# Chunk 1's row transposes moved from TensorE and ScalarE's queue to SyncE's queue, and one subtraction moved ahead of a bias

## The chip, the cores and the metric

One core of one Trainium2 chip runs the whole program. The metric is the time of one execution on the device in microseconds (us). The kernel before took 767.68 us, the median of four runs (767.52 to 768.24). A profile of a further execution is the source of all other times below.

## What is computed

The reference is one transformer layer on a sequence of 2048 rows of 1024 columns in bf16: a layer norm, attention in which each position looks at eight positions at a distance of two, an output projection and a residual sum, then a second layer norm, a bilinear gated block (gate times up, then down) and a residual sum.

```python
S, D, H, Dh, W, dil, F = 2048, 1024, 32, 32, 8, 2, 3584
h  = x + attention(layernorm(x) @ wqkv) @ wo     # 8 keys per position, 2 apart, softmax over the 8
n  = layernorm(h)
h2 = h + ((n @ w_gate) * (n @ w_up)) @ w_down
```

## The kernel before

**Tiling.** The 2048 rows are cut into four chunks (`c` = 0 to 3) of 512 rows, and a chunk into four tiles (`t`) of 128 rows. A tile of rows lies with the rows on the 128 partitions. The matmuls need the normalized rows turned, with the columns on the partitions: `lnT1_c` is that turned copy of one chunk, 128 partitions by 8 blocks by 512 rows. A product of 128 output columns with a chunk is a group of eight 128x512 matmuls (`mm_group`), which the program plans at 1.73 us (`GROUP_US`).

**Order.** [...] The class `Background` holds generators of side work (norms, attention). After each matmul group `bg.step(GROUP_US)` adds that much credit, and the generators emit work and `yield` its planned cost until the credit is used up. A yield of 0.45 that goes away therefore lets the next piece of side work be emitted a little sooner.

**The start.** Chunk 0 is normalized and turned on TensorE (`first_transpose`), and its query, key and value projections begin (`qkv(0, [1, 2])`, then `qkv(0, [3])`, line 489 for the matmuls). In these three blocks of four groups each, the generator `rows_gen` normalizes chunk 1 and then chunk 2. For chunk 1 it also turns the rows. Tiles 0 and 1 go through `transpose_on_array`: eight 128x128 transposes on TensorE into two PSUM tiles `ptb` (line 245), then one copy to SBUF on ScalarE and one on VectorE (line 247). Tiles 2 and 3 go through `transpose` with ScalarE's queue as the issuer: one DMA transpose each (line 236). Right after `qkv(0, [3])` comes `qkv(1, [2])`, whose first matmul needs all four turned tiles of chunk 1. The load of the queries for attention (`load_qk`, line 516) is made to wait for the last turned tile too.

**SyncE's queue.** SyncE issues the loads of weights and rows, and the stores of the projections to DRAM: `qd` for the queries (line 395), `kd` and `vd` for keys and values (line 415). `sg` is the SBUF tile that ScalarE fills from PSUM for each store. [...] The normalized rows live in four buffers (pool `ln`), so that the rows of chunk 2 can only be written when the transposes of chunk 1 have read theirs.

**The down projection.** Late in the kernel the down projections of chunks 0 and 1 are computed by a seven-product scheme: `F11`, `F12`, `F22` are sums of activations, `b12`, `b21`, `t2`, `t4` sums and differences of halves of the down weights, each of 14 blocks of 128x512 in two tiles. `dprod` runs one quarter (`q`) of such a product (14 matmuls, line 1108), `put` adds it to the residual and stores it (line 805). `t_half(dst, x0, x1, a)` subtracts one tile of half the weights on VectorE (line 1101). Beside this, chunks 2 and 3 get their second layer norm: `ln_stat` on VectorE, `rstd_of` on ScalarE (lines 190 and 191), the bias `nbs[3]` on VectorE (line 1351), and then `ln_rows`, one ScalarE pass for each tile (line 1197) with a DMA transpose behind it (line 1198). `zs[q]` are the accumulators that the product with `t4` goes on adding to once `put` has read them.

Of the kernel before, what the change touches and what calls it, by code (L numbers as in the profile page):

```python
# [8 lines left out]
BF = mybir.dt.bfloat16  # L9
# [16 lines left out]
TC = 512  # L26
NCH = S // TC
SUB = TC // 4
KO = D // 128
# [49 lines left out]
def kernel(  # L79
# [11 lines left out]
    nc = tc.nc  # L91
# [8 lines left out]
    lnTp = ctx.enter_context(tc.tile_pool(name="lnT", bufs=3))  # L100
# [5 lines left out]
    psum = ctx.enter_context(tc.tile_pool(name="psum", bufs=8, space=PSUM))  # L106
# [82 lines left out]
    def rstd_of(mv4, rs4, lo, hi):  # L189
        nc.scalar.activation(rs4[:, lo:hi], mv4[:, lo:hi, 1], ACTF.Ln, bias=eps[:])  # L190
        nc.scalar.activation(rs4[:, lo:hi], rs4[:, lo:hi], ACTF.Exp, scale=-0.5)
# [21 lines left out]
    lnTs = {}  # L213
# [3 lines left out]
    class Norm1:  # L217
# [11 lines left out]
        def norm(self, t):  # L229
            self.lns[t] = normalize(xtiles[self.c][t], self.mv4, self.rs4, t)  # L230

        def transpose(self, t, eng=nc.sync):
            c = self.c
            if c not in lnTs:
                lnTs[c] = lnTp.tile([128, KO, TC], BF, tag="lnT", name=f"lnT1_{c}")
            eng.dma_start_transpose(lnTs[c][:, :, bass.ts(t, 128)], self.lns[t][:])

        def transpose_on_array(self, t):
            c = self.c
            if c not in lnTs:  # L240
                lnTs[c] = lnTp.tile([128, KO, TC], BF, tag="lnT", name=f"lnT1_{c}")
            for hf in range(2):
                pt = psum.tile([128, KO // 2, 128], BF, tag="mm", name=f"ptb{c}_{t}_{hf}")
                for kk in range(KO // 2):
                    nc.tensor.transpose(pt[:, kk, :], self.lns[t][:, bass.ts(4 * hf + kk, 128)], ident[:])
                copy = nc.vector.tensor_copy if hf else nc.scalar.copy
                copy(lnTs[c][:, bass.ts(hf, 4), bass.ts(t, 128)], pt[:])

    def rows_gen(n, on_array):
        for t in range(6):  # L250
            if t < 4:
                n.stat(t)
                yield 1.5
            if 0 < t < 5:
                n.norm(t - 1)
                yield 0.55
            if t > 1 and on_array:
                if t < 4:
                    n.transpose_on_array(t - 2)
                    yield 0.45  # L260
                else:
                    n.transpose(t - 2, nc.scalar)

    class NormOnScalar(Norm1):

# [80 lines left out]
    ident = const.tile([128, 128], BF)  # L346
# [131 lines left out]
    xtiles[2] = load_x(2, "x", nc.sync)  # L478
    norm1 = {1: Norm1(1), 2: Norm1(2), 3: NormOnScalar(3)}
    bg.add(rows_gen(norm1[1], True))  # L480
    rows2 = rows_gen(norm1[2], False)
    bg.add(rows2)
    for j in range(4):
# [615 lines left out]
    def sub(dst, x0, x1, eng=nc.vector):  # L1099
        for d, a0, a1 in zip(dst, x0, x1):  # L1100
            eng.tensor_tensor(f16(d[:, 0:NH, :]), f16(a0[:, 0:NH, :]), f16(a1[:, 0:NH, :]), ALU.subtract)
# [25 lines left out]
    b11, b21 = ([wts["dn", n, a] for a in range(2)] for n in ("11", "21"))  # L1127

    def halves(parts, name):
        return [pool.tile([128, KO, TC], BF, tag=tag, name=f"{name}{i}") for i, (pool, tag) in enumerate(parts)]  # L1130
# [37 lines left out]
    def ln_stat(c, t):  # L1168
        stats(hss[c][t], ln2[c][0], t)
# [42 lines left out]
    def t_half(dst, x0, x1, a):  # L1212
        sub([dst[a]], [x0[a]], [x1[a]])
# [58 lines left out]
    t2 = halves(((wpool, "w"), (wpool, "w")), "t2_")  # L1272
# [21 lines left out]
    b21 = halves(((lnTp, "lnT"), (lnTp, "lnT")), "b21r")  # L1294
# [53 lines left out]
    t4 = t2  # L1348
    ln_stat(3, 3)
    rstd_of(ln2[3][0], ln2[3][1], 0, 4)  # L1350
    nc.vector.scalar_tensor_tensor(nbs[3], ln2[3][0][:, :, 0], -1.0, ln2[3][1][:], ALU.mult, ALU.mult)
    t_half(t4, b21, t2, 0)
    l3 = lnTp.tile([128, KO, TC], BF, tag="lnT", name="lnT2_3")
    t_half(t4, b21, t2, 1)
    for q in range(4):
# [162 lines left out]
```

## Time and profile before

| What | Value |
|---|---|
| median of four runs | 767.68 us (767.52 to 768.24) |
| the profiled execution | 768.31 us, of which its span is 766.1 us |
| busy: TensorE, VectorE, ScalarE, GpSimd | 756.6, 626.7, 532.7, 144.6 us |
| granted TensorE clock, as a share of full speed | 0.999 |
| two sets of eight transposes of chunk 1 on TensorE | start at 24.12 and 26.29 us |
| two DMA transposes of chunk 1 from ScalarE's queue | issue from 31.03 us, 2.77 us in all |

All times inside the profile count from the start of the span. A line of a timeline has the start, the duration, the engine, the source line, the operation, the tile written and the tiles read, how many there were, and in brackets how long the engine had idled before and what ended that. A name with a q behind it (SPq, ACTq) is the engine's instruction queue that issues a DMA. In the list of waits the numbers are the total, how often, and the longest, in us. The line of a DMA issue ends with the median time from issue to landing in us.

### The profile page before, as it was taken

How to read it: one execution, taken by the hardware profiler on the slowest of the kernel's cores; microseconds unless marked ns; L12 is line 12 of the kernel's file. 1: busy time of each engine (PE TensorE's matmuls, PEld its weight loads, DVE VectorE, ACT ScalarE, POOL GpSimd, SP SyncE). 2: the span in 40 equal slices, each digit the busy share in tenths (PEclk: the TensorE clock that was granted, in tenths of full speed). 3: DMA queues.
4: the chain of work that ended last, by engine and by line, in shares of the span. 5: the costliest groups of instructions: out<-in, count | busy, mean ns of one | idle time of the engine just before them, and what ended most of it. 6: DMA issues, size and time to landing. Idle time of an engine off the chain costs nothing.

```text
span 766.1 us, 10299 instructions
## 1 busy us (share of the span) xinstructions
PE 756.6 (99%) x3592; PEld 349.3 (46%) x3648; DVE 626.7 (82%) x760; ACT 532.7 (70%) x1012; POOL 144.6 (19%) x155
## 2 busy tenths in 40 slices
PE   8999999999999999999999999999999999999998
PEld 6444444444444444444444444444444444444444
DVE  6789999999999999999999999976454454578862
ACT  4756954556799598996898984846767677788230
POOL 0010000200001000020000001018778677600000
PEclk9999999999999999999999999999999999999999
DMA  8989795967998959879768528684242432830001
GB/s 274 231 246 236 182 290 122 311 189 188 327 346 285 304 175 295 273 238 346 238 216 275 176 96 282 143 204 122 63 110 57 109 91 74 269 117 27 1 28 55
DMA packets 191987, 145.77 MB, mean 190 GB/s; under 512 B 81856, under 2 KB 182080, under 8 KB 189888
## 3 DMA queue, kind: packets, MB, share of 16 engines
q1 hardware_dynamic: 180416, 116.94, 53.8%
q0 software_dynamic: 3728, 22.02, 8.5%
q10 hardware_dynamic: 7792, 6.16, 2.7%
q8 instruction: 28, 0.46, 0.3%
q14 instruction: 23, 0.19, 0.1%
HBM read 111.02 MB, written 27.26 MB: 180 GB/s over the span
## 4 chain that ended last, share of the span: by engine, by line
PE 86%; DVE 5%; ACT 5%; DMA 3%; issue 1%; SPq 0%; ACTq 0%; DVEq 0%
PE ps L489 17%; PE dx L1108 6%; PE pz L847 6%; PE pwu L489 6%; PE py L847 6%; PE pg L489 6%; PE pu L489 6%; PE pwg L489 6%; PE px L847 6%; PE wo L661 4%; PE pv L847 3%; PE dy L1108 3%; PE wo L1162 2%; DMA b21r<-in_B_w_down_dram 2%; PE ez L1108 2%; ACT gs L1087 1%
## 5 line engine op out<-in xcount | busy, mean ns | idle before, releaser
L489 PE MATMUL ps<-lnT,w_qkv 128*128 128x512 bf16 x595 | 131.4, 379 | 0.7
L489 PEld LDWEIGHTS <-w_qkv 128*128 128x128 bf16 (+1 forms) x608 | 59.3, 98 | 70.9
L546 DVE TENSOR_TENSOR prod<-qD,kD 128x4096 bf16<-128x4096 bf16 (+1 forms) x34 | 72.3, 2158 | 3.0 <-DMA kD<-kd 3.0
L594 DVE TENSOR_TENSOR pv<-vD,at 128x4096 bf16<-128x4096 bf16 x32 | 72.4, 2286 | 0.3
L847 PEld LDWEIGHTS <-sw 128*128 128x128 f16 x448 | 43.8, 98 | 52.9 <-issue 0.2
L489 PEld LDWEIGHTS <-w_wg 128*128 128x128 bf16 x448 | 43.8, 98 | 52.9
L489 PEld LDWEIGHTS <-w_wu 128*128 128x128 bf16 x448 | 43.8, 98 | 52.8
L403 ACT CAST sg<-ps 128x512 bf16<-128x512 f32 x72 | 41.5, 584 | 31.0 <-PE ps L489 26.4
L847 PE MATMUL px<-lnT,ws 128*128 128x512 bf16 x212 | 53.1, 379 | 0.6
L489 PE MATMUL pg<-lnT,w_wg 128*128 128x512 bf16 x219 | 52.6, 379 | 0.3
L489 PE MATMUL pwu<-lnT,w_wu 128*128 128x512 bf16 x220 | 52.5, 379 | 0.3
L489 PE MATMUL pu<-lnT,w_wu 128*128 128x512 bf16 x220 | 52.5, 379 | 0.2
L489 PE MATMUL pwg<-lnT,w_wg 128*128 128x512 bf16 x219 | 52.3, 379 | 0.2
L847 PEld LDWEIGHTS <-ws 128*128 128x128 f16 x336 | 32.9, 98 | 39.6
L607 POOL DMA_DIRECT2D od<-oD x4 | 2.2, 542 | 251.3 <-DVE oD L605 251.3
L828 POOL TENSOR_TENSOR sw<-ws 128x512 f16<-128x512 f16 x26 | 30.0, 1154 | 79.5 <-ACT pz L872 47.4
L1108 PEld LDWEIGHTS <-gs 128*128 128x128 f16 (+1 forms) x280 | 27.3, 98 | 33.1 <-DVE gs L1276 0.5
L548 DVE TENSOR_TENSOR prod<-prod 128x4096 bf16<-128x4096 bf16 x16 | 36.6, 2287 | 0.3
L864 ACT COPY py<-px 128x512 f32<-128x512 f32 x28 | 16.0, 570 | 24.7 <-PE px L847 24.7
L831 POOL TENSOR_TENSOR sw<-ws,sw 128x512 f16<-128x512 f16 x26 | 30.6, 1176 | 0.0
L829 POOL TENSOR_TENSOR sw<-sw,ws 128x512 f16<-128x512 f16 x26 | 30.0, 1154 | 2.0
L830 POOL TENSOR_TENSOR sw<-ws 128x512 f16<-128x512 f16 x26 | 30.0, 1154 | 0.0
(371 smaller groups left out, 1575.2 us busy)
## 6 DMA issues: line engine op xcount, KB each, us to landing
w_wg<-in_B_w_gate_dram SPq DMA_DIRECT2D x14, 1024.0 KB, 8.3
w_wu<-in_B_w_up_dram SPq DMA_DIRECT2D x14, 1024.0 KB, 8.5
w_pair<-in_B_w_gate_dram SPq DMA_DIRECT2D x14, 512.0 KB, 4.0
w_pair<-in_B_w_up_dram SPq DMA_DIRECT2D x14, 512.0 KB, 5.2
w_wo<-in_A_wo_dram SPq DMA_DIRECT2D x6, 1024.0 KB, 8.3
w_qkv<-in_A_wqkv_dram SPq DMA_DIRECT2D x5, 1024.0 KB, 9.5
kd<-sg SPq DMA_DIRECT2D x32, 144.0 KB, 4.2
vd<-sg SPq DMA_DIRECT2D x32, 144.0 KB, 3.4
```

The lines of the kernel that those rows point to most:

```text
L403: nc.scalar.copy(sg[:, HB:HB + TC], ps[:])
L489: nc.tensor.matmul(ps[:], lhsT=wt[:, ko, bass.ts(j, 128)], rhs=rhs[:, ko, :], start=(ko == 0), stop=(ko == KO - 1))
L546: nc.vector.tensor_tensor(prod[:, j, ds], qD[:, ds], kD[:, ds, o:o + SUB], ALU.mult)
L548: nc.vector.tensor_tensor(prod[:, :, 0:16], prod[:, :, 0:16], prod[:, :, 16:32], ALU.add)
L594: nc.vector.tensor_tensor(pv[:, j], vD[:, :, o:o + SUB], at[:, w, None, :].to_broadcast((128, DH, SUB)), ALU.mult)
L661: nc.tensor.matmul(ps[:], lhsT=oTs[c][:, kk, t, :], rhs=wts["wo", c, hf][:, kk, :], start=(kk == 0), stop=(kk == KO - 1))
L828: eng.tensor_tensor(sw[:, i, 0], a21, a22, ALU.add)
L829: eng.tensor_tensor(sw[:, i, 1], sw[:, i, 0], a11, ALU.subtract)
L830: eng.tensor_tensor(sw[:, i, 2], a11, a21, ALU.subtract)
L831: eng.tensor_tensor(sw[:, i, 3], a12, sw[:, i, 1], ALU.subtract)
L847: nc.tensor.matmul(ps[:], lhsT=lhs[:, ko, :], rhs=rhs[:, ko, :], start=(fresh and ko == 0), stop=(ko == 3), skip_group_check=not fresh)
L1108: nc.tensor.matmul(ps[:, bass.ds(lo, n)], lhsT=lhs[k][:, bass.ts(q, 128)], rhs=rhs[k][:, bass.ds(lo, n)], start=(fresh and k == 0), stop=( ...
```

## The change

There are two edits. In the first, all four tiles of chunk 1 are turned by DMA transposes that SyncE issues; the transposes on TensorE, their four copies, and ScalarE's two DMA issues go away. In the compiled order SyncE issues the first of them behind the eight query stores of chunk 0, then one key store, then the other three, then the remaining key stores. In the second, the first half of the subtraction that makes `t4` is emitted before the bias `nbs[3]` instead of after it. The line numbers of the changed file are 15 lower from line 254 on.

```diff
-        def transpose(self, t, eng=nc.sync):
+        def transpose(self, t):
             c = self.c
             if c not in lnTs:
                 lnTs[c] = lnTp.tile([128, KO, TC], BF, tag="lnT", name=f"lnT1_{c}")
-            eng.dma_start_transpose(lnTs[c][:, :, bass.ts(t, 128)], self.lns[t][:])
-
-        def transpose_on_array(self, t):
-            c = self.c
-            if c not in lnTs:
-                lnTs[c] = lnTp.tile([128, KO, TC], BF, tag="lnT", name=f"lnT1_{c}")
-            for hf in range(2):
-                pt = psum.tile([128, KO // 2, 128], BF, tag="mm", name=f"ptb{c}_{t}_{hf}")
-                for kk in range(KO // 2):
-                    nc.tensor.transpose(pt[:, kk, :], self.lns[t][:, bass.ts(4 * hf + kk, 128)], ident[:])
-                copy = nc.vector.tensor_copy if hf else nc.scalar.copy
-                copy(lnTs[c][:, bass.ts(hf, 4), bass.ts(t, 128)], pt[:])
-
-    def rows_gen(n, on_array):
+            nc.sync.dma_start_transpose(lnTs[c][:, :, bass.ts(t, 128)], self.lns[t][:])
+
+    def rows_gen(n, turned):
         for t in range(6):
...
-            if t > 1 and on_array:
-                if t < 4:
-                    n.transpose_on_array(t - 2)
-                    yield 0.45
-                else:
-                    n.transpose(t - 2, nc.scalar)
+            if t > 1 and turned:
+                n.transpose(t - 2)
...
     rstd_of(ln2[3][0], ln2[3][1], 0, 4)
+    t_half(t4, b21, t2, 0)
     nc.vector.scalar_tensor_tensor(nbs[3], ln2[3][0][:, :, 0], -1.0, ln2[3][1][:], ALU.mult, ALU.mult)
-    t_half(t4, b21, t2, 0)
     l3 = lnTp.tile([128, KO, TC], BF, tag="lnT", name="lnT2_3")
     t_half(t4, b21, t2, 1)
```

## Prediction

> **What bounds the kernel now.** I read the page first, then TensorE's list of waits, then the chain that ended last, and then the timelines of the engines around the two edits. The page says who the bottleneck is:
>
> ```profile
> ## 1 busy us (share of the span) xinstructions
> PE 756.6 (99%) x3592; PEld 349.3 (46%) x3648; DVE 626.7 (82%) x760; ACT 532.7 (70%) x1012; POOL 144.6 (19%) x155
> ```
>
> TensorE is busy for 99% of the span. So an edit gains only by taking work off TensorE, or by closing a gap in it. TensorE's waits, over the whole span, are these:
>
> ```profile
> PE warm_ps L357 <- DVE warm L343: 1.2, 1, 1.2
> PE pt L444 <- DVE ln L437: 0.8, 1, 0.8
> PE ez L1108 <- DVE hsr L805: 0.7, 1, 0.7
> PE ps L450 <- ACT lnT L445: 0.4, 1, 0.4
> ```
>
> Three of the four lie in the first 8 us. The third is the only one in the remaining 758 us, and the second edit stands just ahead of it. The chain of work that ended last shows what the first edit takes away:
>
> ```profile
> 24.28 0.45 PE ptb L245 x8
> 24.73 1.73 PE ps L489 x8
> 26.45 0.45 PE ptb L245 x8
> ```
>
> The two sets of eight transposes stand in the chain between matmul groups, 0.45 us each; TensorE has no idle time around them.
>
> **Edit 1, what it removes.** Off TensorE: 2 x 0.45 = 0.90 us, on the path. Off ScalarE: two copies of 0.59 us and the issue of two DMA transposes, 2.77 us. Off VectorE: two copies of 0.42 us. The last two engines lose 4.0 and 0.8 us beside TensorE's work, so I count nothing for them.
>
> **Edit 1, what it adds.** Four DMA transposes in SyncE's queue. The first matmul of chunk 1 waits for the last of them, so the question is whether it lands in time. The deadline comes from this row:
>
> ```profile
> 35.37 0.19 PE L379 MATMUL l1psq<-rowbq,ones 128*128 128x64 bf16 x1
> ```
>
> That small matmul is followed by two groups of 1.73 us from 35.40, so chunk 1 starts at 38.85 in this profile; without the 0.90 us it starts at 37.95. SyncE's timeline gives the other side, and under it the landings of the two transposes:
>
> ```profile
> 27.99 0.51 SPq L395 DMA_DIRECT2D qd<-sg  x1
> 54.82 6.62 SPq L236 DMA_TRANSPOSE lnT<-ln  x1
> 65.99 1.32 SPq L236 DMA_TRANSPOSE lnT<-ln  x1
> ```
>
> ```profile
> lnT<-ln SPq DMA_TRANSPOSE x1, 10.9
> lnT<-ln SPq DMA_TRANSPOSE x1, 3.2
> ```
>
> The first row is the eighth query store, the last thing ahead of the transposes; it ends at 28.50 and lands 2.9 us after its issue. SyncE is late there because of earlier loads, not because of TensorE, so I leave 28.5 where it is. The rows to be turned are ready by then: VectorE writes the last of chunk 1 from 27.28 for 0.54 us, and a little sooner without its two copies. The other rows of the timeline are two DMA transposes of chunk 2, the first and the last of four; the second list has their landings in the same order (10.9 us for the one issued at 54.82, 3.2 us for the one at 65.99).
>
> An unhindered transpose takes SyncE 1.32 us to issue. In the compiled order a key store (0.36 us) stands after the first. The last issue starts at about 28.6 + 3 x 1.36 + 0.4 = 33.1 with the small gaps between instructions, and lands 3.2 us later, at 36.3. The lower end is 36.1, with the quickest landing of the profile (3.0). The upper end takes the hindered row: 6.62 us for the first issue, 3.10 for the next (the issue at 61.48), 1.31 for the third, so that the last is issued at 28.6 + 6.62 + 0.4 + 3.10 + 1.31 = 40.0 and lands at 43.2, 5.2 us too late. I take 36.3. The hindered transpose stood behind 2 MB of weights issued in the two microseconds before it (they took 9.1 us to land); ours stand behind stores of 128 KB, the last of which is in DRAM by 30.9. The nearest neighbours are two transposes of the same chunk from ScalarE's queue:
>
> ```profile
> 31.03 2.77 ACTq L236 DMA_TRANSPOSE lnT<-ln  x2
> 35.83 0.19 POOL L516 COPY qD<-lnT 128x1 bf16<-128x1 bf16 x1 [26.63 <-DMA lnT<-ln]
> ```
>
> They were issued in 2.77 us at the same place of the kernel, and GpSimd, which waits for the last, goes on at 35.83, 4.8 us after the first issue. Four at that pace from 28.6, with the store between, give 28.6 + 0.4 + 4 x 1.38 + 1.9 = 36.4, the same. So there are 1.6 us to spare, and the transposes cost TensorE nothing.
>
> [...]
>
> **Who stands behind the new issues.** On SyncE the ninth key store, issued at 30.96 before, goes out at about 34.5. Who waits is the key load for attention (line 519), which needs the sixteenth store: issued at 40.99 before, because ScalarE was still catching up after its 2.77 us of issuing. Without that, ScalarE casts the last group right after TensorE ends it, and the sixteenth store goes out at about 39. The query load waits for the last transpose: 36.3 in place of 35.8. VectorE's rows of chunk 2 wait for the four buffers, hence for the landings; the last would be written at about 37, against 38.84 before. All this lies beside TensorE's matmuls; attention begins at 50.5 before, and I expect it one to two us sooner, which nobody on TensorE waits for.
>
> **Edit 2.** VectorE and TensorE around 490 us:
>
> ```profile
> 489.02 0.21 DVE L187 BATCH_NORM_AGGREGATE mv<-st 128x2 f32<-128x12 f32 x1
> 490.72 0.16 DVE L1351 SCALAR_TENSOR_TENSOR lnroom<-mv,rs 128x4 f32<-128x4 f32 x1 [1.48 <-ACT rs L191]
> 490.80 3.95 DVE L1101 TENSOR_TENSOR t<-b21r,t 128x3584 f16<-128x3584 f16 x2
> 494.67 0.69 DVE L1357 TENSOR_TENSOR ep<-ep,hsr 128x512 f32<-128x512 f32 x1
> 495.46 0.75 DVE L805 SCALAR_TENSOR_TENSOR hsr<-ez,inv_h1d,ep 128x512 bf16<-128x512 f32 x1
> 496.26 12.25 PE L1108 MATMUL ez<-t,a22r 128*128 128x512 f16 x56 [0.74 <-DVE hsr L805]
> ```
>
> VectorE idles 1.48 us until ScalarE has the reciprocal deviations of chunk 3 for the bias. The two halves of the subtraction, one addition and the `put` that frees `zs[0]` are queued behind it, and TensorE waits 0.74 us for that `put`. With the first half ahead of the bias, VectorE starts it at 489.23: its inputs were converted by 485.73. It ends near 491.2, when the deviations (490.69) are there, and no idle time is left. From 490.72 to the end of the `put` at 496.21 the same five pieces take 5.49 us, so they end at 494.72. TensorE would have been free at 496.26 - 0.74 = 495.52. The whole 0.74 us goes, with 0.8 us to spare.
>
> The added wait is the bias's, 0.5 us later (491.2 in place of 490.72). ScalarE's four rows of chunk 3 behind it (4.64 us) end at 496.1 in place of 495.56. They are covered: ScalarE's next work waits for a weight load until 499.29. With that cover gone, 0.5 us would reach the weight sums. What is late next: the second sum of turned rows, which VectorE writes from 508.14 to 509.37; TensorE needs it at 510.94 - 0.74 = 510.2, if VectorE does not move at all. 0.8 us are left.
>
> **The sum.** 0.90 + 0.74 = 1.64 us. The profiled execution took 768.31 us, 2.21 more than its span; its span would become 766.1 - 1.64 = 764.5. The profiled execution is 0.63 above the median of the runs, which I take as the base: 767.68 - 1.64 = 766.04, and I say 766.0. A measurement of this kernel can tell about 0.2%, or 1.54 us, from no change; the sum lies only 0.1 us beyond that.
>
> **Rivals.** *The transposes land too late (slower).* Mechanism: SyncE's issue is held up behind what is in its queue, as at 54.82. Place: the first matmul of chunk 1. Each us after 37.95 costs TensorE one; the gain is used up at 39.6, and from 41.1 on the kernel is slower by more than can be told. At the upper end, 43.2, the time is 766.04 + 5.2 = 771.3. For it: DMA engines are full from 12 to 26 us (share 1.02 from 10 to 20 us, 1.01 from 20 to 30), and VectorE's reduction, ScalarE and SyncE are all behind there. Against it: the share falls to 0.37 from 30 to 32 us, when the loads are in.
>
> *Only one of the two gains arrives.* The first alone gives 766.8, the second alone 766.9. For it: the gap at 496 closes a chain that ran through ScalarE and a weight load of 12.95 us since 466, and margins of 0.8 us lie behind it; or the transposes eat up to 0.9 us. Against it: no other wait of TensorE shows after 8 us.
>
> **How the numbers follow.** Both gains in full: 0.76, of which 0.58 faster beyond the bound and 0.18 within it, since ScalarE's and VectorE's freed time can only add. One gain alone: 0.10, all within the bound. Too late: 0.14, all slower. This gives 0.58, 0.28 and 0.14. The first case alone spans 765.2 to 766.6; the range goes up to 768.0 to take in the single gains and the beginning of lateness, and leaves out most of the slower rival.
>
> **What would show it.** Right: no `ptb` rows, no wait of TensorE for a DMA at 38 us, four transposes issued by SyncE between 28.5 and 34.6, and GpSimd's copy for the query load at about 36.4; VectorE goes from the statistics to the subtraction without a gap near 488, and the 0.7 us wait is off TensorE's list. Wrong: a TensorE wait on `lnT` near 38 us, issues of several us on SyncE at 28 to 34, or a new TensorE wait at 494 to 510.

## The result, and the profile after

| | Before | Changed |
|---|---|---|
| median | 767.93 us (767.52 to 770.66, 54 runs) | 766.38 us (766.10 to 767.91, 36 runs) |
| profiled execution | 768.31 us, span 766.1 | 767.88 us, span 766.0 |

The changed kernel is faster. The ratio of the times is 0.9978 (95% interval 0.9974 to 0.9983). That is 1.69 us of 767.93, with the interval from 1.31 to 2.00; the two medians differ by 1.55. The prediction was 1.64 us. Its 766.0 stands 0.38 us under the measured median, mostly because its base, 767.68 from four runs, is 0.25 us under the median of the 54.

Not all of the gain lies inside the span, the time from the first to the last instruction. By the medians of the runs the span fell from 765.8 us (33 runs) to 764.5 us (36 runs), 1.3 us. The rest of an execution's time, outside the span, fell from 2.16 us (2.09 to 2.24) to 1.86 us (1.81 to 1.91). These 0.3 us are a term that the prediction does not have.

The profiled execution of the changed kernel was not a typical one. Of its 36 runs, 34 lie between 766.10 and 766.54 us; this one took 767.88. Its list of TensorE's waits says where the difference is. The numbers are the total, how often, and the longest, in us:

```profile
PE pwg L474 <- ACT us L730: 1.3, 1, 1.3
PE warm_ps L342 <- DVE warm L328: 1.2, 1, 1.2
PE pt L429 <- DVE ln L422: 1.0, 1, 1.0
PE ps L435 <- DMA w_qkv<-in_A_wqkv_dram: 0.4, 1, 0.4
PE ps L435 <- ACT lnT L430: 0.4, 1, 0.4
```

The wait for the `put` (0.7 us before) is gone. A wait of 1.3 us is new, at the first `pwg` group. The timeline puts it at 298.69 us, far from both edits:

```profile
295.49 1.89 PE L474 MATMUL pu<-lnT,w_wu 128*128 128x512 bf16 x8
298.69 1.67 PE L474 MATMUL pwg<-lnT,w_wg 128*128 128x512 bf16 x7 [1.31 <-ACT us L730]
```

The releaser in the brackets is not the real one: in other profiles the same group begins while ScalarE has yet to write that `us` (in late_bias, below, at 297.20 with the `us` written from 297.97). This group is the first to read the turned rows of chunk 1's second norm. SyncE's timeline shows their four transposes taking 15.01 us to issue (11.44 before); the last was issued at 295.3 and landed 3.1 us later, at 298.4:

```profile
281.59 15.01 SPq L617 DMA_TRANSPOSE lnT<-ln  x4
```

None of the profiles of the six variants below that have no delay built in shows more than 0.3 us there, and they have the same transposes. I therefore leave this stall out of the gain. The two groups in the rows above start 3.20 us apart, where a group takes 1.73: the stall costs this execution 1.47 us, about what it lies above the median (767.88 - 766.38 = 1.50). That the late transposes caused it is read from their landing and was not tested; why their issue took longer stays open.

**Edit 1 in the trace.** The chain that ended last (start, duration, what) no longer has `ptb` between the matmul groups:

```profile
17.90 10.74 PE ps L474 x49
28.64 0.05 issue
28.69 6.21 PE ps L474 x28
34.90 0.03 PE l1psq L364
34.93 4.32 PE ps L474 x20
```

TensorE runs from 17.90 us through the small matmul `l1psq` into chunk 1 without a wait. TensorE's timeline has the same stretch; the first row is of the kernel before, the other two of the changed one:

```profile
17.21 7.07 PE L489 MATMUL ps<-lnT,w_qkv 128*128 128x512 bf16 x31
```

```profile
17.47 17.43 PE L474 MATMUL ps<-lnT,w_qkv 128*128 128x512 bf16 x78
34.76 25.42 PE L474 MATMUL ps<-lnT,w_qkv 128*128 128x512 bf16 x115
```

From the first 128x512 matmul to `l1psq` (35.37 before, 34.73 now) it is 18.16 us before and 17.26 now: the 0.90 us are gone in full. The two groups behind `l1psq` begin at 34.76 and take 1.727 us each, so chunk 1 begins at 38.21. SyncE's timeline has the transposes where the prediction put them:

```profile
28.39 1.34 SPq L236 DMA_TRANSPOSE lnT<-ln  x1
29.83 0.52 SPq L400 DMA_DIRECT2D kd<-sg  x1
30.44 4.11 SPq L236 DMA_TRANSPOSE lnT<-ln  x3
34.65 11.75 SPq L400 DMA_DIRECT2D kd<-sg  x11
```

The last issue is at 33.26. GpSimd, which waits for the last turned tile before it loads the queries and then the keys, tells when it landed:

```profile
37.37 0.19 POOL L501 COPY qD<-lnT 128x1 bf16<-128x1 bf16 x1 [28.32 <-DMA lnT<-ln]
38.17 0.70 POOL L502 DMA_DIRECT2D qD<-qd  x1 [0.61 <-DMA kd<-sg]
46.60 1.06 POOL L504 DMA_DIRECT2D kD<-kd  x2 [7.73 <-DMA kd<-sg]
```

It landed at 37.35, with 0.86 us to spare, half of what was forecast. (Chunk 1 itself begins 0.26 us later than forecast, because TensorE reaches its first 128x512 matmul 0.26 us later in this execution.) The lists of DMA issues of two short windows, around the first transpose and around the last, have the landing times of 3.2 and 4.1 us:

```profile
lnT<-ln SPq DMA_TRANSPOSE x1, 3.2
```

```profile
lnT<-ln SPq DMA_TRANSPOSE x1, 4.1
```

**Edit 2 in the trace.** VectorE's timeline:

```profile
489.86 0.21 DVE L187 BATCH_NORM_AGGREGATE mv<-st 128x2 f32<-128x12 f32 x1
489.98 1.97 DVE L1086 TENSOR_TENSOR t<-b21r,t 128x3584 f16<-128x3584 f16 x1
491.87 0.15 DVE L1337 SCALAR_TENSOR_TENSOR lnroom<-mv,rs 128x4 f32<-128x4 f32 x1
491.94 2.02 DVE L1086 TENSOR_TENSOR t<-b21r,t 128x3584 f16<-128x3584 f16 x1
493.88 0.68 DVE L1342 TENSOR_TENSOR ep<-ep,hsr 128x512 f32<-128x512 f32 x1
494.67 0.75 DVE L790 SCALAR_TENSOR_TENSOR hsr<-ez,inv_h1d,ep 128x512 bf16<-128x512 f32 x1
```

No row has a bracket: VectorE goes from the statistics to the subtraction and on to the `put`, which ends at 495.42. TensorE's rows follow each other without one too, and need that `put` at 496.19:

```profile
484.10 12.25 PE L1093 MATMUL ez<-b,gs 128*128 128x512 f16 x56
496.19 12.25 PE L1093 MATMUL ez<-t,a22r 128*128 128x512 f16 x56
```

From the start of the first product to the start of the second it is 12.09 us. Before, the first product started here:

```profile
483.27 12.25 PE L1108 MATMUL ez<-b,gs 128*128 128x512 f16 x56
```

With the second at 496.26 that is 12.99 us. So the edit took 0.90 us out of the trace, although the bracket of the idle time before said 0.74.

### The profile page after: what moved, and what is told of

Its sections match the earlier page's. It is cut to its first block, busy times and chain, and to the rows that moved or that the text cites. A ratio compares the mean times of both kernels' runs of the same rounds, so it can differ in the third digit from the quotient of the medians.

```text
span 766.0 us, 10272 instructions
## 1 busy us (share of the span) xinstructions
PE 755.6 (99%) x3576; PEld 348.2 (45%) x3632; DVE 625.8 (82%) x758; ACT 531.7 (69%) x1010; POOL 144.3 (19%) x155
## 4 chain that ended last, share of the span: by engine, by line
PE 86%; DVE 8%; ACT 3%; issue 2%; DMA 1%; ACTq 0%; DVEq 0%
PE ps L474 17%; PE dx L1093 6%; PE pz L832 6%; PE pwu L474 6%; PE py L832 6%; PE pwg L474 6%; PE px L832 6%; PE wo L1147 4%; PE pv L832 3%; PE ey L1093 3%; PE ez L1093 3%; PE ex L1093 3%; PE dy L1093 3%; PE pu L474 2%; PE pg L474 2%; DVE prod L531 2%
## 5 line engine op out<-in xcount | busy, mean ns | idle before, releaser
L1093 PEld LDWEIGHTS <-gs 128*128 128x128 f16 (+1 forms) x280 | 27.3, 98 | 33.1 <-DVE gs L1261 0.5
```

What stands on the lines that cost most here:

```text
L1093: nc.tensor.matmul(ps[:, bass.ds(lo, n)], lhsT=lhs[k][:, bass.ts(q, 128)], rhs=rhs[k][:, bass.ds(lo, n)], start=(fresh and k == 0), stop=( ...
```

## The experiments

The medians below belong to three series, in which the kernel before had medians of 767.96 (33 runs), 767.94 (21 runs) and, for late_bias alone, 768.19 us (13 runs). The code cuts are against the changed kernel, except where the text says otherwise.

The table puts the kernels without a built-in delay side by side. Time, span and the time outside the span are medians of the runs; the last two columns are read from the one profile of each kernel: TensorE's time from its first 128x512 matmul to `l1psq`, where edit 1 stands, and the time between the starts of the two products around the `put`, where edit 2 stands.

| Kernel | Time, us | Span | Time outside the span | First 128x512 matmul to `l1psq` | Start of `ez<-b` to start of `ez<-t` |
|---|---|---|---|---|---|
| before (33 runs) | 767.96 | 765.8 | 2.16 | 18.16 | 12.99 |
| only_transposes | 767.10 | 765.2 | 1.87 | 17.27 | 12.77 |
| only_subtraction | 767.55 | 765.4 | 2.16 | 18.16 | 12.09 |
| idle_transposes | 767.16 | 765.3 | 1.86 | 18.16 | 12.09 |
| idle_copies | 766.43 | 764.5 | 2.00 | 17.26 | 12.09 |
| on_scalar_queue | 766.50 | 764.6 | 1.87 | 17.27 | 12.09 |
| late_bias | 766.27 | 764.5 | 1.79 | 17.27 | 12.09 |
| changed | 766.38 | 764.5 | 1.86 | 17.26 | 12.09 |

My theory: the gain is TensorE's own 0.90 us of transposes plus the wait for the `put`, and nothing else counts as long as the four DMA transposes land before chunk 1 begins. The rivals: the gain comes from the time freed on ScalarE and VectorE, or from the queue that now issues; or the transposes are so late that they eat part of it.

### only_transposes: edit 1 alone

```diff
+    nc.vector.scalar_tensor_tensor(nbs[3], ln2[3][0][:, :, 0], -1.0, ln2[3][1][:], ALU.mult, ALU.mult)
     t_half(t4, b21, t2, 0)
-    nc.vector.scalar_tensor_tensor(nbs[3], ln2[3][0][:, :, 0], -1.0, ln2[3][1][:], ALU.mult, ALU.mult)
```

> The change's first edit alone: chunk 1 turned by four DMA transposes from SyncE, the subtraction left behind the bias. Theory (each edit gains what TensorE loses of its path, 0.90 us and 0.74 us, and the two add): 0.90 us below the kernel before, a ratio of 0.9988, and the 0.7 us wait of TensorE for the put is still in its list. Rival (one edit carries the whole gain): either no gain, ratio 1.000, or the whole 1.6 us, ratio 0.998.

Measured: 767.10 us (11 runs), ratio 0.9989 (0.9981 to 0.9998), which is 0.86 us under the kernel before by the medians. Its list of TensorE's waits keeps the `put`, at 0.5 us in this execution:

```profile
PE ez L1093 <- DVE hsr L790: 0.5, 1, 0.5
```

TensorE's stretch is shorter by the 0.90 us of the two sets of transposes, less rounding. But of the 0.86 us by the medians only 0.6 lie in the span; 0.3 lie outside it, and why stays open. So the agreement of 0.86 with 0.90 is in part luck; what may have kept the span from losing all 0.90 stands under Edit 2 below.

### only_subtraction: edit 2 alone

Against the kernel before:

```diff
+    t_half(t4, b21, t2, 0)
     nc.vector.scalar_tensor_tensor(nbs[3], ln2[3][0][:, :, 0], -1.0, ln2[3][1][:], ALU.mult, ALU.mult)
-    t_half(t4, b21, t2, 0)
```

> The change's second edit alone: the first half of the subtraction ahead of the bias, chunk 1 turned as before. Theory: 0.74 us below the kernel before, a ratio of 0.9990; the wait for the put is gone, the two sets of eight transposes on TensorE are still there. Rival (the closed gap opens again as a wait behind it): no gain, ratio 1.000, and a new wait of TensorE between 494 and 511 us.

Measured: 767.55 us (11 runs), ratio 0.9994 (0.9986 to 1.0003). By the medians that is 0.41 us, and the interval holds no change as well as 1.1 us. TensorE's timeline has the gap closed, with 495.60 - 483.51 = 12.09 us between the two starts, as in the changed kernel:

```profile
483.51 12.25 PE L1108 MATMUL ez<-b,gs 128*128 128x512 f16 x56
495.60 4.70 PE L1108 MATMUL ez<-t,a22r 128*128 128x512 f16 x21
```

The mechanism is there, but this run alone doesn't show its size. The same edit on top of edit 1 takes the median from 767.10 to 766.38, 0.72 us. The gap itself was not the same in each execution: in only_transposes the two starts were 12.77 us apart (495.15 - 482.38), so there the edit could bring 0.68.

### idle_transposes: the changed kernel with TensorE's transposes done for nothing

```diff
+                if t < 4:
+                    for hf in range(2):
+                        pt = psum.tile([128, KO // 2, 128], BF, tag="mm", name=f"ptd{t}_{hf}")
+                        for kk in range(KO // 2):
+                            nc.tensor.transpose(pt[:, kk, :], n.lns[t - 2][:, bass.ts(4 * hf + kk, 128)], ident[:])
                 n.transpose(t - 2)
```

> The changed kernel, with the 16 transposes of tiles 0 and 1 put back on TensorE as idle work: they write PSUM tiles that nobody reads, and the DMA transposes do the turning. Theory (of the first edit only TensorE's time counts): 0.90 us of the gain go again, a ratio to the kernel before of 0.9990. Rival (the gain comes from what ScalarE and VectorE no longer do): the time of the changed kernel, ratio 0.998.

Measured: 767.16 us (11 runs), ratio 0.9989 (0.998 to 0.9998); 0.78 us of the gain are lost by the medians. With the DMA transposes in place and only TensorE's 0.90 us given back, the span is 0.8 us longer, and the time outside it stays as in the changed kernel. This is the cleanest price of edit 1: the two kernels differ in TensorE's 16 transposes alone. It also explains most of a difference that looks odd at first. idle_transposes and only_subtraction give TensorE the same work, and their spans are 765.3 and 765.4 us; of the 0.39 us between their times 0.30 lie outside the span.

### idle_copies: the changed kernel with the freed time of ScalarE and VectorE filled

```diff
+    idle = att.tile([128, D], BF, tag="at", name="idle")
...
+                if t < 4:
+                    nc.scalar.copy(idle[:, 0:512], n.lns[t - 2][:, 0:512])
+                    nc.vector.tensor_copy(idle[:, 512:D], n.lns[t - 2][:, 512:D])
                 n.transpose(t - 2)
```

> The changed kernel, with two copies of 128x512 on ScalarE and two on VectorE put back as idle work, into a tile that nobody reads, at the place of the old copies. Theory (only TensorE's time counts): the time of the changed kernel, ratio 0.998. Rival (the freed time of ScalarE and VectorE is part of the gain): up to 1.2 us of ScalarE's time come back, ratio up to 0.9995.

Measured: 766.43 us (11 runs), ratio 0.9982 (0.9973 to 0.9991), the time of the changed kernel. Filling the freed time costs nothing that these runs can tell, as the prediction counted it. The idle copies take 0.62 us each on ScalarE and 0.28 on VectorE; those that were removed took 0.59 and 0.42, so VectorE's time is given back only in part. The issue time removed from ScalarE is tested by the next kernel.

### on_scalar_queue: all four transposes issued by ScalarE

```diff
-            nc.sync.dma_start_transpose(lnTs[c][:, :, bass.ts(t, 128)], self.lns[t][:])
+            (nc.scalar if c == 1 else nc.sync).dma_start_transpose(lnTs[c][:, :, bass.ts(t, 128)], self.lns[t][:])
```

> The changed kernel, but ScalarE issues the four DMA transposes of chunk 1 instead of SyncE. Theory (the gain is TensorE's time; the issuing queue doesn't matter while the tiles land in time): the time of the changed kernel, ratio 0.998, although ScalarE spends some 5.5 us on issuing. Rival (it is SyncE's queue that helps, or ScalarE's evacuations behind the issues come too late): 0.5 us and more above the changed kernel, with a wait of TensorE for a cast of ScalarE near 30 to 40 us.

Measured: 766.50 us (11 runs), ratio 0.998 (0.9971 to 0.9989). The tile lands earlier, at 35.78 by GpSimd's timeline, and 5.6 us of ScalarE's time go into issuing, and neither moves the end:

```profile
35.78 0.19 POOL L501 COPY qD<-lnT 128x1 bf16<-128x1 bf16 x1 [26.67 <-DMA lnT<-ln]
```

So the gain didn't depend on SyncE's queue (766.50 us here, 766.38 with it). It depended on TensorE not doing the work (767.16 in idle_transposes, where it does).

### behind_2mb: two weight loads ahead of the first transpose in SyncE's queue

```diff
             if t > 1 and turned:
+                if t == 2:
+                    pump(6)
                 n.transpose(t - 2)
```

> The changed kernel, with the two weight loads of 1 MB for key and value blocks, which SyncE issues at about 54 us otherwise, issued right before the first transpose of chunk 1. Theory (a transpose's issue is held up behind what is in the queue, as at 54.82 before): the first issue takes some 6.6 us, the last tile lands at about 44 us, TensorE waits some 6 us for it at 38 us, the time is about 772.4, a ratio to the kernel before of 1.006. Rival (the landing depends on the transposes alone): the time of the changed kernel, ratio 0.998.

Measured: 772.39 us (4 runs), ratio 1.0057 (1.0043 to 1.0071). This is the slower rival made real. The 772.4 us that were expected came true by other terms: a first issue of 4.58 us and not 6.6, a stall of some 4.5 us and not 6, and 1.5 us behind the stall that the expectation did not have. SyncE's timeline shows an issue held up for 4.58 us, the next three for 5.37 in all:

```profile
28.45 1.22 SPq L172 DMA_DIRECT2D w_qkv<-in_A_wqkv_dram  x2
29.76 4.58 SPq L236 DMA_TRANSPOSE lnT<-ln  x1
34.44 0.52 SPq L402 DMA_DIRECT2D kd<-sg  x1
35.05 5.37 SPq L236 DMA_TRANSPOSE lnT<-ln  x3
```

The last tile lands at 42.7 us by GpSimd's timeline, and TensorE stalls. Its timeline names ScalarE's `rs` as the releaser; the group is the first to read the turned tiles, and starts 0.1 us after the last lands:

```profile
42.78 1.86 PE L476 MATMUL ps<-lnT,w_qkv 128*128 128x512 bf16 x4 [4.38 <-ACT rs L190]
```

The bracket says 4.38 us; counted from start to start, as for edit 2 above, the stall costs 0.16 us more, 4.54. But the kernel lost 772.39 - 766.38 = 6.01. The windows (their length, then busy time and count of TensorE, its weight loads, VectorE, ScalarE and GpSimd, then the granted clock, the DMA share and GB/s) show the rest:

```profile
42.30:42.50 0.20, 0.00 (x0) 0.00 (x0) 0.20 (x2) 0.12 (x1) 0.00 (x0) 1.00 1.07 258
42.80:45.80 3.00, 2.78 (x7) 1.08 (x9) 2.75 (x8) 2.91 (x12) 0.79 (x2) 0.50 0.80 144
45.95:46.20 0.25, 0.25 (x2) 0.10 (x1) 0.25 (x1) 0.13 (x1) 0.00 (x0) 1.00 0.30 66
```

Finer windows put the granted clock at 0.50 from 42.51 to 45.92, 3.4 us. TensorE works in them from 42.78 on, and its matmuls start 0.43 us apart instead of 0.216. So 3.14 us of work pass at half speed and cost 1.57 us, which is the missing 1.47 within 0.1.

### behind_1mb: one weight load

```diff
             if t > 1 and turned:
+                if t == 2:
+                    pump(5)
                 n.transpose(t - 2)
```

> The same with only one of the two weight loads of 1 MB ahead of the transposes. Theory: the first issue takes about 3.3 us, the last tile lands at about 40.5 us, TensorE waits some 2.5 us, the time is about 768.9, a ratio of 1.001. Rival (the landing depends on the transposes alone): the time of the changed kernel, ratio 0.998.

Measured: 768.41 us (767.86 to 770.58, 10 runs), ratio 1.0004 (0.9995 to 1.0013). One load uses up about the whole gain; the interval holds the time of the kernel before. The hold-up came elsewhere than expected: the first transpose is issued in 1.34 us and not 3.3, the other three take 7.00, and the last tile lands at 40.86 us by GpSimd's timeline (40.5 expected). The profiled execution is the longest of the ten, and TensorE's stall in it is 2.66 us, with the windows behind it:

```profile
40.94 1.87 PE L476 MATMUL ps<-lnT,w_qkv 128*128 128x512 bf16 x4 [2.66 <-DMA lnT<-ln]
```

```profile
40.30:40.55 0.25, 0.00 (x0) 0.00 (x0) 0.25 (x1) 0.17 (x1) 0.00 (x0) 1.00 0.95 214
40.94:43.90 2.96, 2.74 (x7) 1.03 (x9) 2.68 (x9) 2.76 (x12) 0.81 (x2) 0.50 0.68 168
44.05:44.30 0.25, 0.25 (x3) 0.10 (x1) 0.25 (x2) 0.25 (x2) 0.00 (x0) 1.00 0.56 165
```

This execution lost 770.58 - 766.38 = 4.20 us for a stall of 2.66 by the bracket and 2.82 from start to start. Finer windows put the clock at 0.50 from 40.59 to 44.01, again 3.4 us; from 40.94 on that costs 1.5 us, about the rest. Its mean granted clock was 0.997; that of the other nine was 0.999 or 1.0, and eight of them took 767.86 to 768.67. So the clock did not fall like this in them. They have no trace: whether their stalls were as long, and so whether a stall of this length lowers the clock in some executions and not in others, is not shown.

### early_queries: the query load released by the first turned tile

```diff
-    load_qk(0, after=lnTs[1][:, 0, TC - 1:TC])
+    load_qk(0, after=lnTs[1][:, 0, 127:128])
```

> The changed kernel, with the query load for attention released by the first turned tile of chunk 1 instead of the fourth. Theory (the sixteenth key store, issued at about 39.7 us, lands only at 46.6 because it shares the DMA engines with the query load, which begins after the last transpose): the query load is over before, the store lands in about 3 us, attention begins at 47 to 48 us instead of 50.8, the last transposes land later than 37.4, and TensorE has or has not a small wait at 38 us by how much. Rival (the key stores are late for another reason): attention begins at 50.8 as before. The time of the kernel stays within 0.5 us unless the transposes come too late.

Measured in one run: 771.81 us. I meant it to bring attention forward; it made the transposes late. GpSimd's timeline has the 1 MB load issued at 32.28, between the transposes:

```profile
32.28 0.70 POOL L502 DMA_DIRECT2D qD<-qd  x1 [0.61 <-POOL qD L501]
47.35 1.06 POOL L504 DMA_DIRECT2D kD<-kd  x2 [14.37 <-DMA kd<-sg]
```

The list of DMA issues from 32.6 to 33.5 us gives the last two transposes a median of 7.2 us to land, against 4.1 for the last one of the changed kernel, and TensorE waits for them:

```profile
lnT<-ln SPq DMA_TRANSPOSE x2, 7.2
```

```profile
41.96 1.87 PE L474 MATMUL ps<-lnT,w_qkv 128*128 128x512 bf16 x4 [3.79 <-DMA lnT<-ln]
```

Nothing in SyncE's queue had changed: the issues are where they were (30.31 us for the last three, 4.02 in all). One load on another queue was enough. That the transfers share the DMA engines is the likely reason (the DMA share is 1.20 from 32 to 34 us), but this run does not isolate it. Attention did not begin sooner either (51.65 us): the eighth key store, which the key load waits for, was itself issued at 42.36 us instead of 39.66. TensorE's stall is 3.95 us from start to start, and the clock is at 0.50 for 3.4 us here too, from 41.89 to 45.30.

### late_bias: the bias behind the first `put`

```diff
-    nc.vector.scalar_tensor_tensor(nbs[3], ln2[3][0][:, :, 0], -1.0, ln2[3][1][:], ALU.mult, ALU.mult)
...
+        if q == 0:
+            nc.vector.scalar_tensor_tensor(nbs[3], ln2[3][0][:, :, 0], -1.0, ln2[3][1][:], ALU.mult, ALU.mult)
```

> The changed kernel with the bias of chunk 3 emitted only after the first put of the following loop, so that both halves of the subtraction and that put stand ahead of it. My theory of edit 2: the gain is VectorE's time ahead of the put, and ScalarE's four rows of chunk 3 lie hidden behind a weight load until about 499.2 us. Here the bias is written near 495.5 instead of 491.9, the rows end near 500.2, and the conversion of the weight sums starts about 1 us later than in the changed kernel; if 1 us there has cover on TensorE's side, the time is that of the changed kernel, 766.4, with no new wait of TensorE between 496 and 525. Rival: the cover is as thin as the bracket says, and TensorE waits later for what ScalarE writes; then the time is up to 1 us longer, 767.4. The put itself should end a little sooner, near 495.25 in place of 495.4, which nobody waits for.

Measured: 766.27 us (765.92 to 767.69, 9 runs), ratio 0.9978 (0.9968 to 0.9988), the time of the changed kernel. ScalarE's timeline shows the cover taken away: the four rows now run straight into the conversion of the weight sums, which waits for no weight load any more.

```profile
493.95 4.64 ACT L1182 ACTIVATE prodx<-h,lnroom,rs 128x1024 bf16<-128x1024 bf16 x4 [4.14 <-DVE lnroom L1344]
498.49 3.69 ACT L806 ACTIVATE ws<-w_pair,sbgu 128x4096 f16<-128x4096 bf16 x1
```

Counted from the start of the product `ez<-b`, that conversion begins 498.49 - 482.60 = 15.89 us later, against 499.15 - 484.10 = 15.05 in the changed kernel: 0.84 us late, and TensorE's list of waits has nothing beyond the first microseconds. So the 0.5 us by which edit 2 delays the bias had even more cover than the prediction named. Nothing here beats the changed kernel by more than the runs scatter.

## Why the prediction was right, and where it was not

**The sum.** 1.64 us were forecast; 1.55 by the medians and 1.69 by the ratio were measured. Both edits arrived, so the case taken as the likeliest is the one that occurred. That the sum came out so closely is in part luck. The span, which is all that the two terms speak of, fell by 1.3 us, not 1.64; 0.3 us more came off outside the span. Every kernel here in which DMA transposes turn all of chunk 1 has 1.76 to 2.00 us there by the median; the two that turn half of it on TensorE (before, only_subtraction) have 2.14 to 2.16. Why, no run shows.

**Edit 1's 0.90 us** held: TensorE's stretch lost 0.90 us in each profile of the changed kernel's kind, and 0.78 us of the time went again when the same transposes were put back without their use. ScalarE's and VectorE's freed copies were counted at nothing and showed no worth (idle_copies). The remark that freed time "can only add" found nothing to add.

**The landing** was the weak term: 36.3 forecast, 37.35 measured. The issue (33.1 forecast, 33.26 measured) was right; the landing took 4.1 us and not 3.2. The step that failed took the 3.2 us from one transpose of the profile before, and argued that the engines are free with a DMA share that falls to 0.37 from 30 to 32 us. They are not free once the transposes run; already before, with the two from ScalarE's queue, the share is 1.09 from 32 to 34 us. The windows of the changed kernel:

```profile
30.00:32.00 2.00, 2.00 (x11) 0.94 (x10) 0.98 (x5) 1.92 (x8) 0.00 (x0) 1.00 1.03 211
32.00:34.00 2.00, 2.00 (x11) 0.91 (x10) 1.62 (x4) 0.47 (x2) 0.00 (x0) 1.00 1.17 181
34.00:36.00 2.00, 2.00 (x12) 0.91 (x10) 1.84 (x4) 0.95 (x4) 0.00 (x0) 1.00 1.08 208
```

The last three numbers of a row are the granted clock, the DMA share and the rate: the share is 1.03 to 1.17 at only some 200 GB/s. The transposes and the key stores between them are all that was issued there, so they fill the engines themselves. But the share alone does not tell 4.1 us from 3.2. The transpose that served as the model, issued at 65.99 before, was the last of four as well, and its window looks the same:

```profile
66.00:68.00 2.00, 2.00 (x11) 0.89 (x10) 1.97 (x2) 2.00 (x4) 0.00 (x0) 1.00 1.08 208
```

Only the size is shown: the last of chunk 1's four took 4.1 to 4.2 us in the changed kernel, only_transposes, idle_transposes and late_bias alike. The cause stays open. The margin was 0.86 us, not 1.6; it sufficed.

**Edit 2.** The `put` was to have 0.8 us to spare and has 496.19 - 495.42 = 0.77. The size of the gap was taken from the bracket, 0.74; in the traces the distance between the two starts shrank by 0.90. The idle time is counted from the modelled end of the last matmul, 0.379 us after its start, while the next one in a stream starts 0.216 us after it: 0.163 us are missing from each such gap. What the edit brings is 0.4 us alone and 0.7 on top of edit 1, by the medians of the time and of the span alike, and the first of these can't be told from nothing by its interval. The term of 0.74 was read from a single execution, whose span of 766.1 us was 0.3 longer than the median; the one other trace with the gap, only_transposes, has 12.77 - 12.09 = 0.68. So in a typical execution of the kernel before the gap is probably nearer 0.4 than 0.9, an estimate from the spans (765.8 - 765.4) that no second trace of that kernel confirms. Such a gap would also fit edit 1 alone, whose 0.90 us on TensorE brought only 0.6 in the span: the wait for the `put` would have grown by the other 0.3, to about 0.7. Why it should grow stays open.

**What is late next.** The second sum of turned rows was forecast to keep at least 0.8 us: VectorE writes it by 509.21 and TensorE needs it at 510.87, 1.66 us later. VectorE moved with the edit.

**Attention** was forecast one to two us sooner than 50.5; it began at 50.82. The sixteenth store (eight of queries, then the eighth of keys) did go out at 39.66, as forecast (about 39). But the key load could start only at 46.60 (the `kD` row of GpSimd's timeline above), 6.9 us later; before, 46.24 - 40.99 = 5.2. The query load was issued at 38.17 and took 6.4 us to land beside the last key stores; whether it held them up is not settled, since early_queries, which moved it away, delayed the stores' issue instead. The step went from the issue of a store to its landing at an unchanged duration. It cost nothing, since no one on TensorE waits there.

**The slower rival** did not occur, and behind_2mb confirms its mechanism (behind the two loads the first issue took 4.58 us, 1.34 in the changed kernel) and the timing of its upper end (forecast 43.2 us for the last tile, measured 42.7). Its price was too low: "each us after 37.95 costs TensorE one" leaves out what the granted clock did at the end of the stall. The upper end was put at 771.3; behind_2mb, whose last tile landed 0.5 us sooner than that, took 772.39. The windows of behind_2mb, behind_1mb and early_queries all show that clock at 0.50 for 3.4 us. How long TensorE had stood idle when it fell was not the same: in behind_1mb it fell at 40.59, 2.3 us after the end of the last matmul at 38.28; in early_queries it was 3.7 us and in behind_2mb 4.1. What sets the moment and the length, no run shows.

From the first issue at 28.39 us to the last landing at 37.35 the four tiles, 32 blocks of 128x128, took 280 ns a block, beside TensorE's work. The 16 blocks that TensorE turned before took 0.90 us, 56 ns a block, on its path.

## What to carry to other kernels

Where TensorE is the bound for the whole span, price an edit by TensorE's time alone, and treat the engine that takes the work over as a deadline: find the first reader of the result, and keep the landing ahead of it. Take the landing time of a DMA from a place as loaded as the new one will be, with the new transfers themselves counted; here a single 1 MB load next to the transposes cost about what both edits gained or more (2.0 us by the medians on their own queue, 5.4 us in the one run on another). A stall of a few us can be dearer than its length: in all three profiles with one of 2.7 to 4.4 us the granted clock was at 0.50 for 3.4 us around its end, which cost about 1.5 us more. And compare spans as well as times: an edit can move the time outside the span, here by 0.3 us, and a sum of terms inside the span then fits for the wrong reason.

## What was not expected of the hardware

- Four DMA transposes of 128x1024 in a row held the DMA share at 1.03 to 1.17 with 181 to 211 GB/s, from 30 to 36 us of the changed kernel; with two weight loads under way behind_2mb moved 368 and 336 GB/s at shares of 1.10 and 1.06 from 32 to 36 us. In the changed kernel the last of the four took 4.1 us to land, the first 3.2.
- In the three profiles with a stall of 2.7 to 4.4 us the granted clock was at 0.50 for 3.4 us around its end, which cost about 1.5 us on top. It fell 2.3, 3.7 and 4.1 us after TensorE's last matmul had ended. In the other nine executions with one weight load ahead, which have no trace, the mean clock was 0.999 or 1.0.
- The bracket with the idle time of TensorE understated the gap of 0.90 us before the 128x512 matmuls of `ez<-t` by 0.16: it said 0.74.
- The time outside the span is 2.16 us for one kernel and 1.86 for another in every run within 0.1, and 0.3 us of the gain lie there.
